# One more small transfer behind the load of x: four pieces of 16384 bytes on ScalarE's DMA queue, in a decode kernel fed by SyncE's queue

## The chip, the cores and the metric

The kernel runs on one core of one Trainium2 chip. The time is the device time of one execution in microseconds (us), taken from the runs without and with a profile; the span is the time from the first to the last instruction of the profiled execution. The core has five engines with queues of their own: TensorE (PE), VectorE (DVE), ScalarE (ACT), GpSimd (POOL) and SyncE (SP). SP and ACT can issue DMA transfers; all of the core's transfers run on the same 16 DMA engines.

## What is computed

One decode step of a transformer block, for four sequences and one new token each: attention over the last 4096 positions of a cache, and a gated feed-forward. All inputs are bfloat16.

```python
# B, Sq, D = 4, 1, 576; 32 query heads, 16 key heads of 128; caches of 16384 positions
def _A_ref(x, k_cache, v_cache, wq, wo):
    q = (x @ wq) -> [B, 32, 1, 128]
    k = k_cache[:, :, Sk - 4096:, :] ; v = v_cache[:, :, Sk - 4096:, :]   # each key head serves 2 query heads
    p = softmax(q k^T * 128 ** -0.5)
    return (p v) @ wo
def _B_ref(x, W_gate, W_up, W_down):        # F = 4608
    gate = x @ W_gate ; up = x @ W_up
    return (relu(gate) * up) @ W_down
h  = x + _A_ref(layernorm(x), ...)
h2 = h + _B_ref(layernorm(h), ...)
```

## The kernel before

The window of K and V is 16 x 4 heads of one MB each, 67 MB for K and the same for V. The kernel walks over it in 16 *quads*: a quad is four key heads of one sequence, 4 MB of K and 4 MB of V. A quad lies in SBUF as 128 partitions of 32768 bytes. The buffer `pool` has four slots for quads. Every load of the kernel but that of x is issued by SP, in an order written out by hand (`transfers`): wq in two parts, K0, K1, V0, K2, V1, ... V15, then wo, W_gate, W_up and six pieces of W_down. Ahead of each issue SP waits for the instruction that last used the place in `pool`: K for the last transpose of an earlier quad (`TR`), V for the last product with probabilities (`PV`). L273, L278, L283, L285, L292, L295, L297 and L303 are the lines of these loads.

For a quad i, VectorE transposes K in four parts into `kT`, a buffer of its own with `NKT = 4` places of 8192 bytes in each partition (`tr`, L451); each part waits for the load of K and for the scores that last used that place of `kT` (`QK`). TensorE forms the scores of the part (`qk`, matmuls recorded at L513 and L515), VectorE takes the maximum (`rmax`), ScalarE the exponential (L386), VectorE transposes the probabilities (`trp`), and TensorE multiplies them with V (`pv`). The order on each engine is the program's own order; TensorE's part is a loop over pairs of quads.

At the start ScalarE issues the load of x (L339), then waits for the variance of x and takes its root (L340). POOL fills constants, VectorE makes identity matrices and normalises x, TensorE multiplies it with wq, and the result is laid out for the scores. Behind the attention come the product with wo, the second normalisation, gate and up, and the product with W_down, whose last pieces are waited for one after the other.

A transfer's name, `land("x")` for that of x, stands for its semaphore: an instruction with that name among its `deps` waits until all of it has landed. Transfers with different keys have semaphores of their own.

Of the kernel before, what the change touches and what calls it, by code (L numbers as in the profile page):

```python
# [10 lines left out]
BF16 = mybir.dt.bfloat16  # L11
# [138 lines left out]
def bass_sequential_preLN__sliding_block_cached__glu_gated_reglu__decode_kernel(  # L150
# [12 lines left out]
    with ExitStack() as es:  # L163
        cnt = [0]

        def sb(name, shape, dt):
            return es.enter_context(nc.sbuf_tensor(name, shape, dt))

        pool = sb("pool", [128, NSLOT * QUAD], BF16)
        kT = sb("kT", [128, NKT, QUAD // 8], FP32)  # L170
# [74 lines left out]
        S = Sched()  # L245
# [55 lines left out]
        for k, (f0, f1) in enumerate(WD):  # L301
            transfers.append((("wd", k), f"wd{k}", ["ATTN"],
                              lambda e, f0=f0, f1=f1: e.dma_start(  # L303
                                  out=pool[:, f0 * D:f1 * D], in_=B_W_down.rearrange("(p j) n -> p (j n)", j=JJ)[:, f0 * D:f1 * D])))
# [4 lines left out]
        def land(name):  # L309
            return ("L",) + (name if isinstance(name, tuple) else (name,))  # L310
# [26 lines left out]
        def prog_act(S):  # L337
            a = "scalar"
            S.dma(a, lambda e: e.dma_start(out=x_bf[:, :], in_=A_x.rearrange("b s d -> (b s) d")), "x", name=land("x"))  # L339
            S.op(a, lambda e: e.activation(out=st1[:, 14:15], in_=st1[:, 13:14], func=ACT.Sqrt, bias=eps_c[0:B, 0:1], scale=1.0),  # L340
                 deps=["D_VAR", "EPS"], name="A_STD")
            S.op(a, lambda e: e.copy(out=dup[:, :].rearrange("p (r u) -> p r u", u=2),
                                     in_=bass.AP(tensor=ident_b, offset=0, ap=[[128, 64], [1, 64], [0, 2]])), deps=["IDB"], name="DUP")
            S.op(a, lambda e: e.copy(out=col[:, :].rearrange("p (a s) -> p a s", s=NS),
                                     in_=bass.AP(tensor=ident_b, offset=0, ap=[[128, NS], [0, 128], [1, NS]])), name="COL")
# [3 lines left out]
                                           in_=bass.AP(tensor=ident_b, offset=0, ap=[[128, NS], [0, 16], [1, NS], [0, 2]]),  # L349
# [4 lines left out]
                                     in_=bass.AP(tensor=mask, offset=0, ap=[[NHQ, 128], [0, 16], [1, NHQ]])), deps=["M0"], name="SAME")  # L354
            for u in range(2):
                S.op(a, lambda e, u=u: e.activation(out=xn4[:, u, 0:B], in_=pb[STB][:, 0:B], func=ACT.Copy, scale=par[:, u:u + 1]),
                     deps=["XDUP", "PAR2", "XN4Z"], name=f"XN4{u}")
            for k in range(2):
                S.op(a, lambda e, k=k: e.copy(out=q_bf[:, k, :].rearrange("p (x e k) -> p x e k", e=2, k=32),
                                              in_=pb[QB[k]].rearrange("p (x k e) -> p x e k", e=2, k=32)), deps=["QMM"], name=f"QBF{k}")  # L360
            S.op(a, lambda e: e.copy(out=qrep[:, :, :].rearrange("p x (g y) -> p x g y", g=4),  # L361
                                     in_=sc.ap().rearrange("p (g r) -> p g r", g=4)[:, :, 0:128].rearrange("p g (x y) -> p x g y", x=4)),
                 deps=["QREP"], name="D_QR")
# [16 lines left out]
            for i in range(NQUAD):  # L380
                S.op(a, lambda e, i=i: e.activation(out=diag[:, i % 2, :], in_=spot[:, :], func=ACT.Copy, scale=rmx[:, i % 2:i % 2 + 1]),  # L381
                     deps=[("RMAX", i), "SPOT"], name=("DIAG", i))
                deps = [("BIAS", i)]
                if i >= 2:
                    deps.append(("TRP", i - 2))
                S.op(a, lambda e, i=i: e.activation(  # L386
                    out=Pb[:, (i % 2) * 1024:(i % 2 + 1) * 1024], in_=sc[:, (i % 2) * 1024:(i % 2 + 1) * 1024], func=ACT.Exp,
                    scale=SCALE, bias=bias[:, i % 2:i % 2 + 1], accum_out=rs1[:, i:i + 1]),
                    deps=deps, name=("EXP", i), inc=7 if i == NQUAD - 2 else 1)
                if i + 2 < NQUAD:  # L390
                    qzero(i + 2)
            S.op(a, lambda e: e.copy(out=bass.AP(tensor=spread, offset=0, ap=[[16 * H, H], [4 * H + 1, 4], [4, H]]),
                                     in_=bass.AP(tensor=ident_b, offset=0, ap=[[128, H], [0, 4], [1, H]])),
                 deps=["SP0"], name="SPREAD")
            S.op(a, lambda e: e.copy(out=oX[:, :, :].rearrange("p e b -> p (e b)"), in_=pb[0][:, 0:EO * B]), deps=["OSEL"], name="OX")  # L395
            S.op(a, lambda e: e.activation(out=st2[:, 14:15], in_=st2[:, 13:14], func=ACT.Sqrt, bias=eps_c[0:B, 0:1], scale=1.0),
                 deps=["D_VAR2"], name="A_STD2")
            S.op(a, lambda e: e.copy(out=hnT[0:64, 4, 0:B], in_=tpv[0:64, 16:20]), deps=["TP2", "HN4Z"], name="N1")
            S.op(a, lambda e: e.copy(out=hnT[:, 0:4, 0:B], in_=tpv[:, 0:16].rearrange("p (c b) -> p c b", b=B)), name="N2")
            for u in range(2):  # L400
                S.op(a, lambda e, u=u: e.activation(out=hn4[:, u, 0:B], in_=pb[SUB][:, 400:400 + B], func=ACT.Copy, scale=par[:, u:u + 1]),
                     deps=["HDUP"], name=f"HN4{u}")
            for k, (f0, f1) in enumerate(CUTS):
                S.op(a, lambda e, k=k, f0=f0, f1=f1: e.activation(out=gate_sb[:, :, f0:f1].rearrange("p j f -> p f j"), in_=part(0, k, "f j"), func=ACT.Relu),
                     deps=[("GATE", k)], name=("RELU", k))
# [3 lines left out]
        def prog_dve(S):  # L409
# [12 lines left out]
            for k in range(5):  # L422
                w = 1 << k
                S.op(v, lambda e, w=w: e.tensor_scalar(out=num[:, w:2 * w], in0=num[:, 0:w], scalar1=float(w), scalar2=None, op0=ALU.add),
                     deps=["NUM0"] if k == 0 else [("NUM", k - 1)], name=("NUM", k))
            S.op(v, lambda e: e.transpose(out=numT[:, :], in_=num[:, :]), deps=[("NUM", 4)], name="NUMT")
            for k in range(4):
                S.op(v, lambda e, k=k: e.tensor_tensor(out=ident_b[32 * k:32 * k + 32, 32 * k:32 * k + 32], in0=num[32 * k:32 * k + 32, :],
                                                       in1=numT[32 * k:32 * k + 32, :], op=ALU.is_equal),
                     deps=["NUMT", "P0"] if k == 0 else [], name="IDB" if k == 3 else None, signal=k == 3)  # L430
# [4 lines left out]
                 name="PAR2")  # L435
# [6 lines left out]

            def tr(i, j):
                f = 4 * i + j
                deps = [land(("K", i))]
                if f >= NKT:
                    deps.append(("QK", f - NKT))
                x0 = at[("K", i)] + j * (QUAD // 4)
                src = pool[:, x0:x0 + QUAD // 4].bitcast(FP32).rearrange("p (t c k) -> p c t k", c=2, k=32)
                dst = kT[:, f % NKT, :].rearrange("p (c t k) -> p c t k", c=2, k=32)  # L450
                S.op(v, lambda e: e.transpose(out=dst, in_=src), deps=deps, name=("TR", f), inc=3 if f == 5 else 1)  # L451
# [12 lines left out]
            def own(w):  # L464
# [8 lines left out]
                                              in_=bass.AP(tensor=ident_f, offset=0, ap=[[128, 128], [0, 2], [64, 2], [1, NHQ], [NHQ, 8]]),  # L473
                                              axis=AX.X, op=ALU.add), deps=["IDF", "G0"], name="GATH")
            for i in range(NQUAD):
                for j in range(4):
                    tr(i, j)
                    if j == 0 and i > 1 and i % 2 == VLEAD:
                        own(i // 2 - 1)
                rmax(i)  # L480
                fbias(i)
                trp(i)
# [8 lines left out]
                 deps=["RS", "EXT"], name="NORM")  # L491
# [3 lines left out]
            for k, (f0, f1) in enumerate(CUTS):  # L495
                S.op(v, lambda e, k=k, f0=f0, f1=f1: e.tensor_tensor(out=hh[:, :, f0:f1], in0=part(1, k, "j f"), in1=gate_sb[:, :, f0:f1], op=ALU.mult),
                     deps=[("GU", k), ("RELU", k)], name=("HH", k))
            for j in range(2):
                j0, j1 = j * JJ // 2, (j + 1) * JJ // 2
                S.op(v, lambda e, j0=j0, j1=j1: e.transpose(out=hhT[:, j0:j1, :].rearrange("p j b -> p (j b)"),  # L500
                                                            in_=hh[:, j0:j1, :].rearrange("p j f -> p (j f)")),
                     deps=[("HH", len(CUTS) - 1)], name=("HHT", j))
# [3 lines left out]
        def prog_pe(S):  # L506
# [135 lines left out]
            for k, (f0, f1) in enumerate(WD):  # L642
                deps = [land(("wd", k))]
                for f in range(f0, f1):
                    if f % (JJ // 2) == 0:
                        deps = deps + [("HHT", f // (JJ // 2))]
                    for u in range(2):
# [3 lines left out]
                        deps = []  # L651

        progs = [("gpsimd", prog_pool), ("sync", prog_sync), ("scalar", prog_act), ("vector", prog_dve), ("tensor", prog_pe)]
        S.begin(False)
        for _, p in progs:
# [36 lines left out]
```

## Time and profile before

| | before |
|---|---|
| median of 3 runs | 377.70 us (377.58 to 377.77) |
| the profiled execution | 377.95 us |
| its span | 376.6 us |
| PE / DVE / ACT / POOL busy | 307.4 / 226.6 / 53.4 / 6.1 us |
| read from HBM | 159.58 MB, 424 GB/s over the span |
| granted TensorE clock | 0.918 |
| load of a quad, issue to landing (median) | 27.3 us |

The profile is of one execution on the chip. A row names the engine, the line of the kernel, the operation and its tiles; a "q" behind an engine's name (SPq, ACTq) is its sequencer, which issues DMA transfers. All positions in time are counted from the start of the span. "DMA" in the chain of waits means that the chain's next step waited for a transfer to land. Besides the rows, the trace holds a record of every DMA packet with its start, duration, size and queue (not the DMA engine that ran it), and the time of each increment of a transfer's semaphore.

### The profile page before, as it was taken

The numbers are of one execution on the slowest core, as the hardware profiler recorded it, in microseconds if no ns is written. First come the engines' busy times: TensorE is split into PE (matmuls) and PEld (weight loads), VectorE is DVE, ScalarE is ACT, GpSimd is POOL, SyncE is SP. The second block draws the span as 40 slices with busy tenths as digits, with TensorE's granted clock in tenths as the row PEclk, the third lists the DMA queues.
The fourth block names the chain that finished last, engine by engine and source line by source line (L and its number), as shares of the span: only waits on it lengthen the run. The fifth ranks groups of instructions, "written<-read, shape, count | busy, mean of one in ns | idle before, by whom it ended". The sixth has DMA issues, their size and how long they took to land.

```text
span 376.6 us, 2757 instructions
## 1 busy us (share of the span) xinstructions
PE 307.4 (82%) x1454; PEld 74.0 (20%) x778; DVE 226.6 (60%) x165; ACT 53.4 (14%) x140; POOL 6.1 (2%) x16
## 2 busy tenths in 40 slices
PE   0439999959995999599959996899679977986677
PEld 0102221212121212022201221122112211222214
DVE  8255849494839492949475758675677658222230
ACT  2231220202020202002200211021102010101020
POOL 6000000000000000000000000000000000000000
PEclk9959999989998999589976999899989998996988
DMA  8999999999999999999999999999999999999995
GB/s 335 445 444 432 404 445 445 425 412 442 442 421 421 442 445 432 407 442 445 432 411 439 445 432 414 435 445 432 414 435 445 432 418 435 433 421 435 442 399 237
DMA packets 6501, 159.66 MB, mean 424 GB/s; under 512 B 728, under 2 KB 864, under 8 KB 1632
## 3 DMA queue, kind: packets, MB, share of 16 engines
q1 hardware_dynamic: 6488, 159.59, 98.8%
q8 instruction: 3, 0.05, 0.1%
q14 instruction: 2, 0.02, 0.0%
q10 hardware_dynamic: 8, 0.00, 0.0%
HBM read 159.58 MB, written 0.00 MB: 424 GB/s over the span
## 4 chain that ended last, share of the span: by engine, by line
DMA 60%; DVE 27%; PE 11%; ACT 1%; SPq 1%; issue 0%; DVEq 0%
DMA pool<-in_A_k_cache_dram 55%; DVE kT L451 20%; DMA pool<-in_B_W_down_dram 5%; DVE acc L468 4%; PE sc L513 3%; PE sc L515 3%; DVE P L465 2%; PE val L513 2%; PE val L515 2%; PE pb L513 1%; DVE o_bf L489 0%; ACT L386 0%; DVE probT L462 0%; DVE rmx L454 0%; ACT P L386 0%
## 5 line engine op out<-in xcount | busy, mean ns | idle before, releaser
L451 DVE STREAM_TRANSPOSE kT<-pool 128x2048 f32<-128x2048 f32 x64 | 142.7, 2279 | 20.2 <-DMA pool<-in_A_k_cache_dram 20.1
L513 PE MATMUL sc<-kT,qz 128*128 128x512 bf16 x256 | 109.2, 426 | 40.3 <-DVE kT L451 40.2
L513 PE MATMUL val<-pool,probT 128*64 128x512 bf16 (+2 forms) x344 | 111.2, 374 | 3.1 <-DMA pool<-in_B_W_down_dram 3.1
L515 PE MATMUL sc<-kT,qz 128*128 128x512 bf16 x256 | 108.3, 423 | 0.0
L515 PE MATMUL val<-pool,probT 128*64 128x512 bf16 x272 | 103.1, 379 | 0.0
L513 PEld LDWEIGHTS sc<-kT,qz 128*128 128x128 bf16 x256 | 26.3, 103 | 149.5 <-DVE kT L451 77.1
L513 PEld LDWEIGHTS val<-pool,probT 128*64 128x64 bf16 (+1 forms) x344 | 34.1, 107 | 89.1 <-issue 77.6
L454 DVE TENSOR_REDUCE rmx<-sc 128x1 f32<-128x1024 f32 x16 | 19.6, 1225 | 38.5 <-PE sc L515 38.5
L381 ACT ACTIVATE diag<-spot,rmx 128x16 f32<-128x16 f32 x16 | 4.9, 307 | 242.5 <-DVE rmx L454 242.5
L462 DVE STREAM_TRANSPOSE probT<-P 128x1024 bf16<-128x1024 bf16 x16 | 19.9, 1245 | 20.5 <-ACT P L386 20.5
L386 ACT ACTIVATE P<-sc,bias 128x1024 bf16<-128x1024 f32 x16 | 17.8, 1115 | 18.7 <-DVE bias L457 18.7
L375 ACT COPY qz<-qrep 32x128 bf16<-32x128 bf16 x64 | 18.8, 293 | 0.6
L457 DVE TENSOR_REDUCE bias<-pb 128x1 f32<-128x16 f32 x16 | 2.8, 175 | 22.0 <-PE pb L513 22.0
L465 DVE TENSOR_TENSOR P<-val,mask 128x1024 f32<-128x1024 f32 x8 | 9.5, 1190 | 10.6 <-PE val L515 10.6
L468 DVE TENSOR_REDUCE acc<-P 128x128 f32<-128x1024 f32 x8 | 15.2, 1898 | 0.3
L513 PE MATMUL sc<-pool,oX 128*4 128x288 bf16 x32 | 9.4, 324 | 0.4 <-ACT oX L395 0.4
L515 PE MATMUL sc<-pool,oX 128*4 128x288 bf16 x32 | 9.4, 324 | 0.0
L525 PE MATMUL pb<-ident_b,xn_bf 4*128 4x4 bf16 (+1 forms) x5 | 0.4, 179 | 10.7 <-DVE xn_bf L419 10.7
L492 DVE TENSOR_TENSOR h_row<-sc,x_bf 4x576 f32<-4x576 f32 x1 | 0.7, 746 | 11.0 <-PE sc L515 11.0
L513 PE MATMUL sc<-col,foe 4*128 4x512 bf16 x16 | 6.3, 397 | 1.2 <-ACT qrep L361 1.2
L513 PEld LDWEIGHTS pb<-diag,same 128*128 128x128 f32 x32 | 4.8, 188 | 10.0 <-ACT diag L381 10.0
L513 PE MATMUL pb<-diag,same 128*128 128x16 f32 x32 | 6.3, 273 | 0.0
(103 smaller groups left out, 79.1 us busy)
## 6 DMA issues: line engine op xcount, KB each, us to landing
pool<-in_A_k_cache_dram SPq DMA_DIRECT2D x16, 4096.0 KB, 27.3
pool<-in_A_v_cache_dram SPq DMA_DIRECT2D x16, 4096.0 KB, 27.3
pool<-in_A_wo_dram SPq DMA_DIRECT2D x1, 4608.0 KB, 18.4
pool<-in_B_W_gate_dram SPq DMA_DIRECT2D x1, 4608.0 KB, 19.9
pool<-in_B_W_up_dram SPq DMA_DIRECT2D x1, 4608.0 KB, 23.2
pool<-in_A_wq_dram SPq DMA_DIRECT2D x1, 4096.0 KB, 12.6
pool<-in_B_W_down_dram SPq DMA_DIRECT2D x1, 2016.0 KB, 13.7
pool<-in_B_W_down_dram SPq DMA_DIRECT2D x1, 1296.0 KB, 16.5
```

Source lines behind the costliest of these rows:

```text
L375: S.op(a, lambda e, src=src, dst=dst: e.copy(out=dst, in_=src), deps=deps, name=("QZ", i) if g == 3 else None, signal=g == 3, inc=8 if i = ...
L381: S.op(a, lambda e, i=i: e.activation(out=diag[:, i % 2, :], in_=spot[:, :], func=ACT.Copy, scale=rmx[:, i % 2:i % 2 + 1]), deps=[("RMAX", ...
L386: S.op(a, lambda e, i=i: e.activation(out=Pb[:, (i % 2) * 1024:(i % 2 + 1) * 1024], in_=sc[:, (i % 2) * 1024:(i % 2 + 1) * 1024], func=ACT ...
L451: S.op(v, lambda e: e.transpose(out=dst, in_=src), deps=deps, name=("TR", f), inc=3 if f == 5 else 1)
L454: S.op(v, lambda e: e.tensor_reduce(out=rmx[:, i % 2:i % 2 + 1], in_=sc[:, (i % 2) * 1024:(i % 2 + 1) * 1024], axis=AX.X, op=ALU.max), dep ...
L457: S.op(v, lambda e: e.tensor_reduce(out=bias[:, i % 2:i % 2 + 1], in_=pb[TPB][:, 16 * (i % 2):16 * (i % 2) + 16], axis=AX.X, op=ALU.min), ...
L462: S.op(v, lambda e: e.transpose(out=pT[i % NPT], in_=Pb[:, (i % 2) * 1024:(i % 2 + 1) * 1024]), deps=[("EXP", i)] + ([("PV", i - NPT)] if ...
L465: S.op(v, lambda e: e.tensor_tensor(out=own_sb[:, :].rearrange("p (x d) -> p x d", d=DH), in0=val[:, :].rearrange("p (x d) -> p x d", d=DH ...
L468: S.op(v, lambda e: e.tensor_reduce(out=acc[:, w, :], in_=own_sb[:, :].rearrange("p (x d) -> p d x", d=DH), axis=AX.X, op=ALU.add), deps=[ ...
L492: S.op(v, lambda e: e.tensor_tensor(out=h_row[:, :], in0=attn, in1=x_bf[:, :], op=ALU.add), deps=["ATTN", land("x")], name="H")
L513: return e.matmul(o, lhsT=l, rhs=r, start=start, stop=stop, skip_group_check=skip)
L515: return e.add_instruction(mybir.InstMatmult(name=nc.get_next_instruction_name(), start_tensor_calc=start, stop_tensor_calc=stop, bass_ski ...
```

## The change

Right behind the load of x, ScalarE issues one more transfer. It reads the first eight rows of wq (8 x 8192 bytes) as four pieces of 16384 bytes, and writes them to partitions 0, 8, 16 and 24 of `kT`, over its first two places. The first transpose into `kT` waits for it in addition; it and the second one then overwrite these bytes, and nothing reads them.

```diff
         def prog_act(S):
             a = "scalar"
             S.dma(a, lambda e: e.dma_start(out=x_bf[:, :], in_=A_x.rearrange("b s d -> (b s) d")), "x", name=land("x"))
+            S.dma(a, lambda e: e.dma_start(
+                out=kT[0:32:8, 0:2, :].rearrange("p f n -> p (f n)").bitcast(BF16), in_=A_wq[0:8, :].rearrange("(a c) n -> a (c n)", c=2)),
+                "stagger", name=land("stagger"))
             S.op(a, lambda e: e.activation(out=st1[:, 14:15], in_=st1[:, 13:14], func=ACT.Sqrt, bias=eps_c[0:B, 0:1], scale=1.0),
                  deps=["D_VAR", "EPS"], name="A_STD")
...
             def tr(i, j):
                 f = 4 * i + j
-                deps = [land(("K", i))]
+                deps = [land(("K", i))] + ([land("stagger")] if f == 0 else [])
                 if f >= NKT:
                     deps.append(("QK", f - NKT))
```

## The prediction

> **What bounds the kernel now.** I read the share of the span by engine, then the DMA queues, the chain that ended last, the work by stages, and the waits of SP. Besides these views I used the trace's single records of DMA packets (start, duration, size, queue) and of semaphore increments; I name them where I use them.
>
> The queues of the page first:
>
> ```profile
> q1 hardware_dynamic: 6488, 159.59, 98.8%
> q8 instruction: 3, 0.05, 0.1%
> q14 instruction: 2, 0.02, 0.0%
> q10 hardware_dynamic: 8, 0.00, 0.0%
> HBM read 159.58 MB, written 0.00 MB: 424 GB/s over the span
> ```
>
> SP's queue (q1) fills the sixteen DMA engines for 98.8% of the span. The 8 packets of q10 are the load of x: by the records four of 1152 bytes and four of 4 bytes (semaphore increments), so a transfer of four rows runs on four engines. q8 and q14 fetch instructions through the same engines; they matter below.
>
> The work by stages (PE, PEld, DVE, ACT, POOL busy, then clock, DMA share, GB/s):
>
> ```profile
> 24.00:120.00 96.00, 84.65 (x348) 19.26 (x179) 67.47 (x42) 14.20 (x36) 0.00 (x0) 0.94 1.00 431
> 120.00:220.00 100.00, 89.20 (x356) 19.94 (x183) 67.74 (x42) 12.92 (x35) 0.00 (x0) 0.90 1.01 434
> 220.00:320.00 100.00, 84.15 (x347) 19.21 (x179) 66.76 (x42) 11.86 (x31) 0.00 (x0) 0.95 1.00 431
> ```
>
> No stage of the attention loop leaves the DMA engines idle. The packets of 32768 bytes take 1217.7 ns on average and 1211 at the least (4224 records), which is 16 x 32768 / 1.2177 = 430.6 GB/s: the rate of the stages. The stream is bounded packet by packet on each engine.
>
> The end of the chain:
>
> ```profile
> 353.06 0.33 SPq L303
> 353.43 0.43 SPq L303
> 353.90 0.43 SPq L303
> 354.38 18.94 DMA pool<-in_B_W_down_dram
> 373.36 0.70 PE val L513 x7
> 374.08 0.68 PE val L513 x5
> 374.78 0.42 DVE out_sb L503
> ```
>
> The last piece of W_down ends the kernel. Was the stream ever dry? The small up load is issued at 337.74 and takes 24.1 us, to 361.8; the down loads are issued from 353.06, 8.8 us before that. A K or V load takes 27.3 us from issue to landing where its bytes need 8 x 1.2177 = 9.7 us. So the queue always holds more, and a delay of about a microsecond in compute is hidden.
>
> Only one thing remains: when does the **slowest** engine finish? The increments answer it. The last down piece lands on the sixteen engines at 0 to 0.31 us (ten engines), 0.53, 0.57, 1.01, 1.75, 1.87 and 1.97 us after the first. Three engines are late. At each of them the records show a fetch: q8 packets of 16384 bytes at 24.4, 329.7 and 362.4 us of the span stand in a gap of 0.96, 1.08 and 1.07 us in one engine's q1 packets, and the next packet there is 0.47 us longer than its like. Each costs its engine 1.43 to 1.55 us. Later loads keep the delay: the latest engine is 1.69 us behind the first at 102.7 us and still at 297.0 us.
>
> **The change part by part.** The four pieces are shaped as x is: four rows, so four engines, one packet of 16384 bytes each (64 KB in all).
>
> (1) Bytes on four engines. By size a piece costs half of a 32768-byte packet: 1.213 / 2 = 0.61 us on each of the four engines, on the other twelve nothing. The nearest row for a strange packet inside a full stream is q8's, of the same size: 1.43 to 1.55. I take 0.61, because the source and target are those of ordinary loads and the packet arrives when the stream begins (SP's first load is issued at 0.73 us, and this one at about 1.3). Both ends are kept: 0.61 to 1.55. A gain from the bytes themselves is excluded: nothing is taken away.
>
> (2) Where this goes. An engine that gets 0.61 us more and is not one of the three late ones still finishes in front of them: room is 1.97 - 0.57 = 1.40 us for twelve engines and 1.97 - 1.01 = 0.96 for the thirteenth. So the end moves by 0 unless one of the late three is among the four. Which are they? By the packet records, q1 begins on the sixteen engines one after the other within 0.49 us. I followed the late engines back, packet to packet (the next begins 3 to 4 ns ahead of the end of the last); all three lead to engines that began tenth or later. Ties of a nanosecond leave this uncertain. If four rows go to the engines that are served first, the late ones are spared. The Trainium skill, "DMA: Bandwidth & Descriptors", section "Why a DMA increments its semaphore by 16 and not by 1", says that a transfer on k engines uses the lowest-numbered k; the same page, "Latency and other measured facts", says that engines 7 and 15 are usually the slower ones. No record here carries an engine's number; by both rules the end would move by 0.
>
> (3) The issue on ScalarE's queue:
>
> ```profile
> 0.73 0.55 ACTq L339 DMA_DIRECT2D x_bf<-in_A_x_dram  x1
> 1.38 1.28 ACT L340 ACT_TABLE_LOAD   x1 [1.38 <-POOL xn L327]
> 8.43 0.29 ACT L340 ACTIVATE st<-st,eps_c 4x1 f32<-4x1 f32 x1 [5.77 <-DVE st L415]
> ```
>
> A second issue of 0.55 us pushes the table load from 1.38 to about 1.93, over at 3.2; the next ACT work waits until 8.43 for DVE. 5.77 us of idle time cover it: cost 0. Without that cover it would be 0.55 us. x is issued ahead of it and is not delayed.
>
> (4) The new wait on DVE, ahead of the first transpose into kT (L451). That transpose starts at 23.64, when K0 lands; the pieces are issued at 1.3 and need 1 to 2 us. The semaphore is long up, and one passed wait is left. DVE's next transposes queue behind it, and PE's first scores behind those; cost 0 to some hundredths of a us, covered as below.
>
> (5) The first loads on the four engines: wq and K0 land up to 0.61 us later (1.55 at the far end). Q's matmuls, V0's issue (16.81) and the first transpose (23.64) move with them. What comes late is the issue of the load freed at 49.22, which lands 24.4 us after its issue where its bytes need 9.7. 14.7 us of queue cover it. Without that queue the whole 0.61 would count.
>
> Sum: profiled span 376.6, plus 0 = 376.6; with the 1.35 us that lie around the span, 377.95 as profiled. The runs shown have a median of 377.70, 0.25 lower; against them the forecast is 377.7. A change of 0.2%, 0.76 us, is about what a measurement of this kernel can tell from none.
>
> **The rivals.**
>
> *A late engine is among the four* (slower). Place: the last landing at 374.4. It decides as soon as one of the three carries a piece. Price 0.61 by bytes: 378.3, within 0.2%. At q8's price 1.55: 379.25. It counts as slower above 0.76; the middle, 1.08, gives 378.8. For it: drawn blind, four of sixteen miss all three late engines in only 12 x 11 x 10 / (16 x 15 x 14) = 39% of cases. Against it: the tracing back in (2).
>
> *Shifting four engines by half a packet loosens the stream* (faster). If the engines hinder each other because they walk in step, packets could fall from 1217.7 towards 1211 ns: 264 packets of 32768 bytes on each engine x 6.7 ns = 1.8 us at most; half of it gives 376.8. For it: all engines keep one pace over 194 us. Against it: that pace is the same for engines at 0, 0.5, 1.0 and 1.7 us of offset, and single engines already walk far out of step without going faster. The Trainium skill, "DMA: Bandwidth & Descriptors", section "Latency and other measured facts", reports that copies with a row pitch of 4 MiB halve in rate, and infers streams in lock-step on the same channel. K's heads lie 16384 x 128 x 2 bytes = 4 MiB apart, but the trace has 431 to 434 GB/s and nothing near a half; so hardly any of that is there to be won.
>
> *The change doesn't do what it says*: the transfer is spread over all sixteen engines. Then 4 KB each, 1.213 / 8 = 0.15 us on every engine, the late ones too: 377.85.
>
> **How the numbers follow.** Hidden behind the late engines: 0.56, at 377.7. A late engine hit: 0.26, at 378.3 to 379.25. Loosened stream: 0.12, at 376.8 in the middle. Spread over sixteen: 0.06, at 377.85. Slower by over 0.2%: 0.18 of the 0.26, as most prices between the ends lie above 0.76, and 0.05 of the first case, for the first stage's irregular packets (127 of 992 above 1230 ns between 25 and 101 us) growing with the shift: 0.23. Faster: 0.12. Within 0.2%: 0.65. The range takes half of the loosened case at the bottom, 377.0, and the greater part of the hit case at the top, 378.9.
>
> **What would show it.** q10 has 16 packets instead of 8, four of them of 16384 bytes, in the first 4 us. The increments of K1 and later loads show four engines 0.6 us further back and the same three last. The first transpose starts up to 0.6 us later, the last landing stays at 374.4. I am wrong if the last landing moves: by 0.6 or more, then a late engine was hit; forward, with packets nearer 1211 ns, then the stream was loosened; or if the fetches fall on other engines or cost something else.

## The result, and the profile after

| | before | after |
|---|---|---|
| median of 22 runs each | 377.75 us (377.55 to 379.48) | 378.44 us (378.02 to 380.39) |
| ratio after / before | | 1.0022, 95% interval 1.0012 to 1.0031 |
| the profiled execution, its span | 377.95, 376.6 us | 378.52, 377.2 us |
| last landing of W_down, from the span's start | 374.39 us | 374.99 us |
| first landing of K0, spread over the sixteen engines | 23.12 us, 0.50 us | 23.76 us, 1.55 us |

The change costs 0.69 us. That is little, but the interval of the ratio leaves no room for "no change": the forecast of 377.7 was wrong, and the time lies in the upper part of its range. In what follows a difference is that of the medians of one comparison; the ratio is taken round by round on one chip. The two mostly agree within 0.2 us, but not always: the ratio says 0.6 us where the medians say 0.32 (sixteen pieces), and 1.6 us where they say 1.11 (partitions 0 to 3).

The page of after first, its DMA queues:

```profile
q1 hardware_dynamic: 6488, 159.59, 98.7%
q10 hardware_dynamic: 16, 0.07, 0.1%
q8 instruction: 3, 0.05, 0.1%
q14 instruction: 2, 0.02, 0.0%
HBM read 159.65 MB, written 0.00 MB: 423 GB/s over the span
```

The stream is the same 6488 packets. q10 has eight packets more: by the records four of 16384 bytes and four increments. The change does what it says, on four engines.

The same three stages of the attention loop (PE, PEld, DVE, ACT, POOL busy, then clock, DMA share, GB/s):

```profile
24.00:120.00 96.00, 84.18 (x349) 19.20 (x179) 67.02 (x41) 15.30 (x40) 0.00 (x0) 0.97 1.00 431
120.00:220.00 100.00, 88.48 (x356) 19.82 (x183) 68.75 (x42) 12.93 (x35) 0.00 (x0) 0.91 1.00 431
220.00:320.00 100.00, 84.51 (x339) 19.13 (x175) 66.54 (x41) 11.85 (x31) 0.00 (x0) 0.91 1.01 433
```

Nothing has changed here: the rate is 431 to 433 GB/s, as before. The time is lost before 24 us, and then carried to the end. The end of the chain of waits of after (start, length, what; us):

```profile
354.70 0.33 SPq L303
355.08 0.43 SPq L303
355.55 0.43 SPq L303
356.03 17.93 DMA pool<-in_B_W_down_dram
374.00 1.36 PE val L516 x12
375.38 0.42 DVE out_sb L506
```

The chain has the same members. The last twelve matmuls end at 375.36 instead of 374.76, and the span is 0.6 us longer. What moved is the last landing, by 0.60 us, and nothing was added behind it. The increments of this last piece come at 0 to 0.43 us (nine engines), 0.75, 1.56, 1.69, 1.70, 1.76, 1.81 and 2.11 us after the first: one engine alone is now last, where three late ones stood close together before.

The start of the same chain, before and then after:

```profile
1.65 21.96 DMA pool<-in_A_k_cache_dram
23.64 2.32 DVE kT L451
```

```profile
1.65 23.66 DMA pool<-in_A_k_cache_dram
25.34 2.32 DVE kT L454
```

The first load of K lands for the first transpose 1.70 us later, not the 0.61 that the pieces' bytes explain. The rates of the first stage, 4 to 10 us of the span, before and then after, in the view of the work by stages:

```profile
4.00:10.00 6.00, 0.00 (x0) 0.00 (x0) 5.72 (x17) 1.00 (x3) 2.60 (x7) 1.00 1.02 437
```

```profile
4.00:10.00 6.00, 0.00 (x0) 0.00 (x0) 5.72 (x17) 1.00 (x3) 2.60 (x7) 1.00 0.98 377
```

The last number falls from 437 to 377 GB/s, while the DMA share hardly falls: the engines are as busy, but move less. The records say how. The pieces' packets begin at 5.88, 6.21, 6.22 and 7.32 us and take 611, 611, 611 and 796 ns. The 32 KB packets of wq that begin between 5.7 and 8.1 us take 1264 to 1765 ns, one 2055, where most take 1213 in before: 0.59 us of extra time on the mean of the sixteen engines, called the **stall** below. It is not on the four engines alone: the first landing of the last piece of W_down, which is that of an engine without a piece, comes at 372.88 instead of 372.43. Engines that carry a piece are behind by more: K0's offsets are 0 to 0.40 us on twelve engines, then 0.71, 0.95, 1.07 and 1.55.

ScalarE's queue and engine in the timeline of after:

```profile
1.35 0.68 ACTq L340 DMA_DIRECT2D kT<-in_A_wq_dram  x1
2.12 1.28 ACT L343 ACT_TABLE_LOAD   x1 [2.12 <-POOL xn L327]
8.43 0.29 ACT L343 ACTIVATE st<-st,eps_c 4x1 f32<-4x1 f32 x1 [5.03 <-DVE st L418]
```

The issue pushes the table load to 2.12, and the next work still begins at 8.43. Nothing is lost here.

### The profile page after: what moved, and what is told of

The parts are those of the page before. It is cut to its first block, busy times and chain, and to the rows that moved or that the text cites. A ratio compares the mean times of both kernels' runs of the same rounds, so it can differ in the third digit from the quotient of the medians.

```text
span 377.2 us, 2759 instructions
## 1 busy us (share of the span) xinstructions
PE 308.5 (82%) x1454; PEld 74.1 (20%) x778; DVE 226.6 (60%) x165; ACT 53.4 (14%) x140; POOL 6.1 (2%) x16
## 3 DMA queue, kind: packets, MB, share of 16 engines
q1 hardware_dynamic: 6488, 159.59, 98.7%
## 4 chain that ended last, share of the span: by engine, by line
DMA 54%; DVE 29%; PE 14%; ACT 1%; SPq 1%; issue 0%; DVEq 0%
DMA pool<-in_A_k_cache_dram 49%; DVE kT L454 21%; DMA pool<-in_B_W_down_dram 5%; PE sc L516 4%; DVE acc L471 4%; PE sc L518 4%; PE val L516 3%; DVE P L468 2%; PE val L518 2%; DVE probT L465 1%; ACT P L389 1%; PE pb L516 1%; DVE o_bf L492 0%; ACT L389 0%; DVE rmx L457 0%
## 5 line engine op out<-in xcount | busy, mean ns | idle before, releaser
L474 DVE STREAM_TRANSPOSE qT<-q_bf 128x1024 bf16<-128x1024 bf16 x1 | 1.2, 1245 | 9.8 <-ACT q_bf L362 9.8
## 6 DMA issues: line engine op xcount, KB each, us to landing
pool<-in_B_W_down_dram SPq DMA_DIRECT2D x1, 2016.0 KB, 12.7
```

Source lines behind the costliest of these rows:

```text
L474: S.op(v, lambda e: e.transpose(out=qT[:, :], in_=q_bf[:, :, :].rearrange("p k x -> p (k x)")), deps=["QBF1"], name="D_QT")
```

## The experiments

In the diffs the two operands of the added transfer stand on lines of their own, and only what changes is shown. All are against the changed kernel, unless "before" is named. For each run the text gives the difference from before, the ratio with its interval, and the last landing (374.39 in the profiled execution of before, 374.99 after). A landing or a stall is that of one profiled execution. The stall is the mean, over the sixteen engines, of the time by which the 32 KB packets of q1 exceed 1213 ns while the pieces run.

**First: is it the bytes, their place, or the wait?** The source was the first suspect for the stall: the pieces read rows of wq that the stream reads at the same time.

*Another source*, outside the window of K:

```diff
-in_=A_wq[0:8, :].rearrange("(a c) n -> a (c n)", c=2)
+in_=A_k_cache[0, 0, 0:256, :].rearrange("(a c) d -> a (c d)", a=4)
```

> The four pieces have the same size, targets, queue and wait as in the change, but are read from 64 KB of the K cache outside the window, which no other load reads, instead of the first rows of wq. Theory 1 (late engine: the pieces hold up only their four engines, two of which also fetch instructions on q14 and so finish last): nothing changes, 0.6 to 0.7 us above before (378.4). Theory 2a (all sixteen engines stall while the pieces run, because both queues read wq at once): the packets of 32768 bytes between 5 and 9 us stay near 1213 ns instead of 1400 to 1750, and the first engine's landing of K0 comes 0.6 us earlier than with the change; time 0.0 to 0.3 us above before. Theory 2b (any second queue with data stalls all): as with the change, 378.4, packets up to 1700 ns.

Measured: 378.33, +0.62, ratio 1.0013 (1.0005 to 1.0022); last landing 374.79. The stall is nearly gone (0.15 us), and the rate of the first stage recovers to a good part:

```profile
4.00:10.00 6.00, 0.00 (x0) 0.00 (x0) 5.72 (x16) 1.00 (x3) 2.60 (x7) 1.00 0.99 415
```

Yet the end is nearly as late as after. So here it is not the stall of all sixteen that costs the time at the end; K0's spread, 1.05 us, shows single engines still behind by more than 0.61. And the pieces did not run together this time (two at 6.0 and 6.3, two at 7.1 us), so that the source wasn't the only difference.

*Sixteen pieces of 4096 bytes*, the same 64 KB:

```diff
-out=kT[0:32:8, 0:2, :], in_=A_wq[0:8, :].rearrange("(a c) n -> a (c n)", c=2)
+out=kT[0:128:8, 0, 0:1024], in_=A_wq[0:8, :].rearrange("a (c n) -> (a c) n", c=2)
```

> The same 64 KB of wq on the same queue, in sixteen pieces of 4096 bytes to sixteen partitions, so that all sixteen engines share them. Theory 1 (late engine): each engine gets 4096 / 32768 of 1.21 us, 0.15 us, the late ones too; the end moves by 0.15, time 377.9, and the spread of K0's landing stays near 0.4 us. Theory 2a and 2b (stall of all while 64 KB pass): the stall is that of the change, 0.4 to 0.6 us on all engines, time 378.2 to 378.4, with packets above 1400 ns in the wq stage.

Measured: 378.03, +0.32, 1.0016 (1.0005 to 1.0026). The stall is 0.08, K0's spread 0.43, the last landing 374.38. Against the next run, whose pieces have almost no bytes, the landing is 0.16 later, which is the price by bytes (0.15); the medians say twice that and the ratio four times, so its size stays open. The spread of the pieces does away with the single late engines, but not with the bytes.

*Four pieces of 64 bytes*, with the same wait and the same issue:

```diff
-out=kT[0:32:8, 0:2, :], in_=A_wq[0:8, :].rearrange("(a c) n -> a (c n)", c=2)
+out=kT[0:32:8, 0, 0:16], in_=A_wq[0:8:2, 0:32]
```

> Four pieces of 64 bytes instead of 16384, same queue, partitions and wait; only the bytes are gone. Theory 1 and theory 2a: no measurable difference from before, within 0.15 us of 377.75. Theory 2b in the form that the second queue itself (its descriptors, its wait) costs, not its bytes: 0.3 to 0.7 us above before. It also shows what the issue on ScalarE's queue and the wait ahead of the first transpose cost by themselves; expected 0.

Measured: 377.69, -0.02, 1.0001 (0.9992 to 1.0010); last landing 374.22. Neither the issue, nor the wait, nor four more packets cost anything. All of the change's cost is in the bytes or in where they go.

*Pieces of twice the size*:

```diff
-out=kT[0:32:8, 0:2, :], in_=A_wq[0:8, :].rearrange("(a c) n -> a (c n)", c=2)
+out=kT[0:32:8, 0:4, :], in_=A_wq[0:16, :].rearrange("(a c) n -> a (c n)", c=4)
```

> Four pieces of 32768 bytes, twice the change, into all four places of the buffer. Theory 1 (late engine): the four engines lag by 1.2 to 2 us at K0 instead of 0.4 to 1.2, the last of them is 0.6 us later at the end than with the change: 379.0 to 379.2, the first engines' landings unmoved against the change. Theory 2 (stall of all): the first engine's landing of K0 moves too, by about another 0.6 us, and the time is 379.0 or more with a spread at the end that grows less than 0.6.

Measured: 379.32, +1.61, 1.0046 (1.0033 to 1.0059); stall 0.88, last landing 375.65. Doubling adds 0.92, which is more than the 0.61 us by bytes.

**Second: how many engines, and when?**

*Two pieces*, from K's cache:

```diff
-out=kT[0:32:8, 0:2, :], in_=A_wq[0:8, :].rearrange("(a c) n -> a (c n)", c=2)
+out=kT[0:16:8, 0:2, :], in_=A_k_cache[0, 0, 0:128, :].rearrange("(a c) d -> a (c d)", a=2)
```

> Two pieces of 16384 bytes instead of four, read from the K cache outside the window as in the run with the other source, so they use two DMA engines. Revised theory 1: what ends the kernel later is the piece on an engine that later also runs an 8 KB instruction fetch (q14); in the runs so far both such engines were among the four. If neither is among the first two, the end stays within 0.15 us of before (377.7 to 377.85), and two increments of K0 lie 0.6 to 1 us back while the last three of the last landing are the engines of the 16 KB fetches. If one is among them, 378.2 to 378.4, the same as with four pieces. Rival (any second-queue data on any engine costs the end in proportion): half of the 0.62 us of four pieces, 378.0.

Measured: 377.88, +0.16, 1.0005 (0.9996 to 1.0014); last landing 374.23. Not told apart from no change, although one engine with an 8 KB fetch is among the two, for which 378.2 to 378.4 was expected. K0's offsets show 1.04 and 1.11 on two engines. Between the loads that land at 72 and 81 us one of them meets an 8 KB instruction fetch (q14): followed packet by packet, it loses 0.69 us and goes from 1.06 to 1.75. The other engine with such a fetch carries no piece and goes from 0.46 to 1.46. At the end the first is at 1.85, only just in front of the late ones at 1.89 to 2.01.

*The same pieces, issued later*, behind two activations on ScalarE, at 11.78 instead of 1.35 us, so that they run in the stream of K0, at 15.7 to 17 us (the diff is against before, the wait ahead of the first transpose is that of the change):

```diff
             S.op(a, ...)   # the two activations that write xn
+            S.dma(a, lambda e: e.dma_start(
+                out=kT[0:32:8, 0:2, :], in_=A_wq[0:8, :].rearrange("(a c) n -> a (c n)", c=2)),
+                "stagger", name=land("stagger"))
```

> The transfer of the change, rows 0 to 7 of wq, but issued on ScalarE behind L359, at about 12.5 us of the span, so that it runs while K0 streams and not while wq does. Revised theory 1 (late engine): the four engines still lag by 0.6 to 1.1 us and the end comes 0.5 to 0.65 us above before, 378.2 to 378.35, as with the other source. Theory 2a (both queues reading wq make all sixteen stall): packets stay at 1213 to 1300 but on the four engines, and the first landing of the later K loads is 0.3 to 0.4 us earlier than with the change. If the stall of all engines comes from the transfer's place at the start rather than from wq, it is gone here as well, and only the run with other rows tells.

Measured: 378.35, +0.63, 1.0017 (1.0008 to 1.0026); stall 0.43, last landing 374.82. By then the stream had left wq. So "both read wq" falls, and so does "it is the first packets of the stream".

*Other rows of wq*:

```diff
-in_=A_wq[0:8, :]
+in_=A_wq[256:264, :]
```

> The change, but the four pieces are read from rows 256 to 263 of wq instead of 0 to 7, at the same time of the span. Theory 2a in the form same tensor (lock-step with the stream of wq): packets of all engines near 1500 ns on average between 5 and 9 us, as in the change, 378.4. In the form same rows (both read the same 64 KB): no such stall, as with the other source; time still 378.3 through the late engine. The late engine is expected in both.

Measured: 378.45, +0.73, 1.0017 (1.0008 to 1.0026); stall 0.41, last landing 374.88. The same cost from rows that the stream reads at another time: the source's place is not it.

*Before, with the last piece of W_down in two transfers*, partitions 0 to 87 and 88 to 127, so that the late engines might be spared:

```diff
+        PARTS = {len(WD) - 1: ((0, 88), (88, 128))}
-                                  out=pool[:, f0 * D:f1 * D], ...
+                                  out=pool[p0:p1, f0 * D:f1 * D], ...
```

> The kernel before, without the pieces; only the last piece of W_down (1152 bytes for each of 128 partitions) is split in two transfers, partitions 0 to 87 and 88 to 127, which should run on 11 and on 10 engines instead of 16. If the end is set by the engines of the 16 KB instruction fetches and these are not among the eleven, those engines are spared 8 packets of about 53 ns, the others carry 12 instead of 8: the last landing comes 0.3 to 0.4 us earlier, 377.3 to 377.45. If a late engine is among the eleven: 0.1 to 0.3 us later than before, 377.8 to 378.0. If the end isn't set by the slowest engine at all: no change, 377.7.

Measured: 378.05, +0.33, 1.0003 (0.9993 to 1.0013): no gain. The last piece now lands early, at 373.58 and 373.78, but the two in front of it land at 373.71 and 374.38 instead of 373.32 and 374.03, and the last 14 matmuls wait for these. It gave something else: the first part has increments of eleven engines, and they end at 373.58, while the three with the 16 KB fetches are at 373.99 to 374.38 with the piece before: none of the three is among the eleven. So a transfer of four rows misses these three, if it takes the first of the same engines: this step of the prediction held.

**Third: the law of sizes, the source again, and taking load off the late engines.**

*Half the size*:

```diff
-out=kT[0:32:8, 0:2, :], in_=A_wq[0:8, :].rearrange("(a c) n -> a (c n)", c=2)
+out=kT[0:32:8, 0, :], in_=A_k_cache[0, 0, 0:128, :].rearrange("(a c) d -> a (c d)", a=4)
```

> Four pieces of 8192 bytes, read from the K cache outside the window; half of the bytes of the run with the other source. Revised theory 1 (late engine, with a threshold): the two engines that also run the 8 KB fetches lie about 0.75 and 1.1 us behind the first without any piece, and half a piece adds 0.3 to 0.5 us; 1.1 + 0.5 = 1.6 is less than the 1.75 to 1.97 of the engines with the 16 KB fetches, so the end moves by less than 0.15 us: 377.65 to 377.85. Rival (the cost goes with the bytes): half of 0.62, 378.0.

Measured: 377.81, +0.10, 0.9998 (0.9989 to 1.0007); last landing 374.42. For these targets, pieces below some size between 8 and 16 KB are hidden.

*A third source*, wo:

```diff
-in_=A_wq[0:8, :].rearrange("(a c) n -> a (c n)", c=2)
+in_=A_wo.rearrange("r n -> (r n)")[0:32768].rearrange("(a c) -> a c", a=4)
```

> Four pieces of 16384 bytes as in the change, read from the first 64 KB of wo, a weight that no other load reads at that time. If the stall of all sixteen engines comes from pieces out of wq alone, packets stay as with the K cache (0.15 us of excess on average over the engines between 4.5 and 8 us); if from pieces out of any weight, 0.4 to 0.6 us of excess. Revised theory 1 expects the end at 378.3 to 378.45 in both cases, since the engine that ends last is one with a piece.

Measured: 378.39, +0.68, 1.0016 (1.0006 to 1.0025); stall 0.38. (Its profiled execution lies 1.5 us above its median, so only its start is read; the last landing in it, 374.54, does not explain that time.) wo is read by the stream 300 us later, and the cost is the same as from wq.

*Twice the size from K's cache*:

```diff
-out=kT[0:32:8, 0:2, :], in_=A_wq[0:8, :].rearrange("(a c) n -> a (c n)", c=2)
+out=kT[0:32:8, 0:4, :], in_=A_k_cache[0, 0, 0:512, :].rearrange("(a c) d -> a (c d)", a=4)
```

> Four pieces of 32768 bytes, read from the K cache outside the window, so that they surely overlap each other in time. Revised theory 1: an engine with piece and 8 KB fetch lies 1.1 plus 1.3 to 1.8 us behind the first, 2.4 to 2.9, and the end comes 0.7 to 1.2 us above before, 378.4 to 378.9. If the stall of all sixteen needs only that four pieces run at once, it shows here too (first landing of K0 0.4 us or more later than with the tiny pieces) and the time is that of the doubled change, 379.3; if it needs wq as source, it doesn't.

Measured: 379.60, +1.89, 1.0046 (1.0032 to 1.0060); stall 0.91, last landing 375.86; more than expected. With longer pieces the overlap is certain, and the stall from K's cache is as large as from wq (0.88). The source is out. The increments show what is late at the end: between the loads that land at 62 and 82 us, offsets of 1.48 and 1.65 become 2.35 and 2.46. The jump is that of the two 8 KB fetches of q14; without bytes (the run with 64 bytes a piece) the same jump leads to 0.73 and 1.09. **Both engines with an 8 KB fetch carry a piece.**

*Before, with wq's last part in three transfers* (partitions 0 to 63, 64 to 107, 108 to 127), to move bytes between engines at the start:

```diff
+        SHARE = ((0, 64), (64, 108), (108, 128))
-            lambda e, o: e.dma_start(out=o, in_=A_wq[512:576, :]...)
+            ... for h, (p0, p1) in enumerate(SHARE): e.dma_start(out=pool[p0:p1, ...], in_=...[p0:p1, :])
```

> The kernel before, without pieces; the first load (the last 64 rows of wq, 4096 bytes for each of 128 partitions) is split by partitions 0 to 63, 64 to 107 and 108 to 127, which should run on 16, 11 and 10 engines: engines 11 to 15 then move 4 packets of 159 ns instead of 8, the first ten 10. If the three engines of the 16 KB fetches are among the last five, they lie 0.6 us less behind and the others 0.3 us more: the last landing comes 0.3 to 0.6 us earlier, 377.2 to 377.45. If the end isn't set by these engines, or the split costs the start more than it brings: 377.7 or later.

Measured: 379.46, +1.75, 1.0047 (1.0033 to 1.0062). It says nothing of the balance: the issues put SP's next load of wq from 1.20 to 2.30 us, and that delay of the whole stream covers anything else.

*The same split for a late load*, the small part of W_up, in before and in after:

```diff
+        SHARE = ((0, 64), (64, 108), (108, 128))
+        for h, (p0, p1) in enumerate(SHARE):
+            transfers.append((("wu4", h), f"wu4_{h}", made[2], ... out=pool[p0:p1, wu4:wu4 + HALF], ...
```

> The kernel before, without pieces; only the small load of W_up (4608 bytes for each of 128 partitions) is split by partitions 0 to 63, 64 to 107 and 108 to 127, so that engines 11 to 15 move 4 packets of 178 ns instead of 8 and the first ten 10; it is queued 8 us ahead of its turn, so the start and the queue are not touched. Theory (the slowest engine sets the end, and in before these are the three with the 16 KB fetches, none of them among the first eleven): the three lie 0.7 us less behind, the others 0.36 more; the last landing moves from 1.75 to 1.97 behind the first engine's old place to 1.3 to 1.5: 377.25 to 377.5. If the slowest engine doesn't set the end, 377.7; if the split has a side effect as at the tail, 377.8 to 378.1.

> The same split of W_up's small load, but in the kernel with the change. Theory: here the last engine is one of the four with a piece, the lowest-numbered ones, and the split gives it two packets of 178 ns more: 0.36 us later than the change, 378.7 to 378.9. The sign is opposite to that in before. If the engines with the 16 KB fetches ended last here as well, it would be 0.3 to 0.5 us earlier than the change, 377.95 to 378.15.

Measured: 380.99, +3.17, 1.0081 (1.0068 to 1.0095) in before; 382.58, +4.76, 1.0126 (1.0110 to 1.0141) in after. Both are far from what was expected. The stage in which this load runs, in before and then in the split version of before:

```profile
356.50:363.50 7.00, 6.79 (x109) 1.49 (x41) 0.00 (x0) 2.80 (x7) 0.00 (x0) 0.76 0.98 412
```

```profile
356.50:363.50 7.00, 5.97 (x86) 1.46 (x38) 0.69 (x2) 2.48 (x7) 0.00 (x0) 0.76 0.97 246
```

412 GB/s become 246 at the same DMA share: the sign of the stall again, without any piece. In this stage the packets of 4608 bytes take 350 ns (median, at most 547) instead of 179. A load split by partitions ran at little more than half the rate. That pointed at the target.

The split version of after says one more thing. Up to this load it is the changed kernel, with the same pieces from the same rows, and yet its stall is 0.19 instead of 0.59. Its pieces begin at 6.29, 7.04, 7.07 and 7.09 us, those of after at 5.88, 6.21, 6.22 and 7.32. With one set of targets the stall therefore varies from execution to execution.

**Fourth: the targets.**

*Three pieces*, at partitions 0, 8 and 16:

```diff
-out=kT[0:32:8, 0:2, :], in_=A_wq[0:8, :].rearrange("(a c) n -> a (c n)", c=2)
+out=kT[0:24:8, 0:2, :], in_=A_k_cache[0, 0, 0:192, :].rearrange("(a c) d -> a (c d)", a=3)
```

> Three pieces of 16384 bytes from the K cache outside the window, so on three engines. Two pieces gave 0.16 us above before, four gave 0.62. Theory: with two pieces one engine of the 8 KB fetches is hit, with four both; the one that comes last in the four-piece run decides. If it is the third, 378.2 to 378.35 as with four; if it is the fourth, 377.85 to 377.95 as with two. A cost in proportion to the bytes would give 378.15.

Measured: 377.82, 0.00, 1.0000 (0.9991 to 1.0009); last landing 374.14. Both expectations were too high. One engine is 0.94 behind at K0, and one with an 8 KB fetch ends at 1.28, still in front of the late three (1.75 to 1.77). It takes the fourth piece to push an engine past them.

*The same pieces to partitions 0, 4, 8 and 12*; size, source, queue, issue and wait as in the change:

```diff
-out=kT[0:32:8, 0:2, :]
+out=kT[0:16:4, 0:2, :]
```

> The change with other target partitions: 0, 4, 8 and 12 instead of 0, 8, 16 and 24; bytes, source, queue, engines and wait are the same. Theory of the writing side (the pieces and the running stream meet in groups of four partitions, each of which one engine fills in the quad loads; the first four engines then own 0 to 3, 4 to 7, 8 to 11 and 12 to 15): no engine meets another, the packets of the sixteen stay near 1213 ns while the pieces run, each piece costs its engine 0.61 us by its bytes, an engine with piece and 8 KB fetch ends at 1.1 + 0.6 = 1.7 us behind the first, no later than the engines of the 16 KB fetches (1.75 to 1.97), and the time is 377.7 to 377.9: what the prediction forecast for the change itself. The Trainium skill, SBUF: State Buffer, section on the DMA port swizzle, gives these groups of four partitions and a port for each. Rival (four large pieces at once stall all engines wherever they are written): 378.3 to 378.45, as with the change.

Measured: 377.77, -0.05, 1.0002 (0.9989 to 1.0014).

```profile
4.00:10.00 6.00, 0.00 (x0) 0.00 (x0) 5.72 (x17) 1.00 (x3) 2.60 (x7) 1.00 1.00 426
```

426 GB/s against 377. The four pieces take 611 ns each, of the 97 packets of 32 KB that begin between 5 and 12.7 us 93 take 1213 and the longest 1284, and K0's offsets are 0.59, 0.66, 0.67 and 0.68 on four engines: near the price by bytes, 0.61, as the prediction had it. (Its profiled execution is 0.7 us above its median, with slower packets between 16 and 62 us; only the start is read.)

*The same pieces to partitions 0, 1, 2 and 3*:

```diff
-out=kT[0:32:8, 0:2, :]
+out=kT[0:4, 0:2, :]
```

> The change with the four pieces written to partitions 0, 1, 2 and 3. Theory of the writing side: four engines and the stream's own writer meet in one group of partitions; the pieces take about four times as long as by their bytes, 2.4 us, and the four engines lag by 1.5 to 2.5 us at K0: with the 8 KB fetches 2.6 to 3.6 at the end, time 378.6 to 379.6. Rival (target doesn't matter): 378.3 to 378.45, as with the change.

Measured: 378.93, +1.11, 1.0042 (1.0026 to 1.0058); last landing 375.41.

```profile
4.00:10.00 6.00, 0.00 (x0) 0.00 (x0) 5.72 (x17) 1.00 (x3) 2.60 (x7) 1.00 0.86 350
```

The worst of the three: the pieces take 725 to 973 ns, the sixteen packets of q1 beside them 2207 to 2536, and the stall is 1.24 us. The time was expected, the path was not: the pieces were to take 2.4 us and their engines to be 1.5 to 2.5 us behind at K0; they are 0.67 to 1.15 behind, and it is all sixteen that are late. One thing besides the targets differs: the issue takes 0.26 instead of 0.68 us, and the pieces begin at 3.40 us, beside the first 32 KB packets of wq, not at 5.9.

The Trainium skill, "SBUF — State Buffer", section "Door 1: The DMA port swizzle (why `[64,N]` ≈ `[32,N]`)", says that four neighbouring partitions share a port of the memory, sixteen ports in all, and that a transfer's rate hangs on how many of them its partitions reach; "DMA: Bandwidth & Descriptors", section "The descriptor swizzle", gives each engine one port in a transfer to all partitions. If the four engines are the first four, 0, 4, 8 and 12 are their own ports; of 0, 8, 16 and 24 three are other engines' ports; 0 to 3 are all one. The stalls, 0.05, 0.59 and 1.24 us, come in that order, and the 350 ns against 179 above agree with it too. No record carries a port, so that the runs show the dependence on the targets, and the ports are the Trainium skill's explanation of it. They do not settle when the stall is large: it is 0.15 to 0.59 in the runs with 0, 8, 16 and 24, and three pieces to 0, 8 and 16, all begun at 7.05 to 7.09 us, took 611 ns each with a stall of 0.05. The times depend on the targets more steadily than the stalls: five versions with four pieces of 16384 bytes to 0, 8, 16 and 24 cost 0.62 to 0.73 us, the one to 0, 4, 8 and 12 nothing that is measured.

*Twice the size to 0, 4, 8 and 12*:

```diff
-out=kT[0:32:8, 0:2, :], in_=A_wq[0:8, :].rearrange("(a c) n -> a (c n)", c=2)
+out=kT[0:16:4, 0:4, :], in_=A_wq[0:16, :].rearrange("(a c) n -> a (c n)", c=4)
```

> Four pieces of 32768 bytes from wq to partitions 0, 4, 8 and 12. Theory of the writing side: 1.21 us on four engines and nothing on the others; an engine with piece and 8 KB fetch ends at 1.1 + 1.2 = 2.3 us behind the first, 0.35 to 0.55 us after the engines of the 16 KB fetches: 378.05 to 378.35, the first landing of K0 at 23.1 to 23.4 us. Rival (target doesn't matter): as the doubled change, 379.3, with the first landing of K0 at 24.2.

Measured: 378.26, +0.44, 1.0016 (1.0006 to 1.0025); stall 0.06, pieces 1213 to 1224 ns, last landing 374.75. The end of its chain:

```profile
356.44 17.26 DMA pool<-in_B_W_down_dram
373.74 1.37 PE val L516 x12
375.14 0.41 DVE out_sb L506
```

Almost without a stall, 1.21 us on four engines do show at the end, where 0.61 did not. No rule of collisions is needed for this: only the room of an engine that the prediction left out of account.

**The sum that fits.** With 64 bytes a piece the late three land at 374.22 at the latest, and the later of the two engines with an 8 KB fetch at 372.48 + 1.18 = 373.65 (first landing and its offset). Room: 0.57 us. What the pieces cost this engine is read at K0, 350 us ahead of the end; 23.46 stands for the landing of K0 with 64 bytes a piece, a value about the middle of the sixteen (23.31 to 23.66), so that a sum holds to some 0.1 us. The end should be the later of two: the late three, and 373.65 plus that cost:

| targets, bytes a piece | cost on that engine | it lands, by the sum | the late three land | last landing, measured |
|---|---|---|---|---|
| 0, 8, 16, 24; 16384 (after) | 1.37 (K0 at 23.76 + 1.07, against 23.46) | 375.02 | 374.57 to 374.69 | 374.99 |
| 0 to 3; 16384 | 1.73 (24.49 + 0.7, against 23.46) | 375.38 | to 375.39 or 375.41 | 375.41 |
| 0, 4, 8, 12; 32768 | 1.21 (by bytes) | 374.86 | to 374.21 | 374.75 |
| 0, 4, 8, 12; 16384 | 0.61 (by bytes) | 374.26 | | the median is that of before |

For after, 1.07 is the offset of the engine that goes to 2.06 between 72 and 82 us. The engine was picked by what it does later, so the table shows that the numbers agree and is no forecast.

The late three carry no piece, as far as the increments can be followed, and yet the stall moves them. In after they land at 374.57 to 374.69; they would have been last, 0.30 us after before's 374.39, even without the fourth engine, which adds another 0.30. With targets 0 to 3 the stall makes the whole price: the late three are as late as the engine of the sum, so this row is no test of it. The row with 32768 bytes is: there the late three stand where they do with 64 bytes, and the engine with piece and fetch alone passes them.

## Why the prediction was wrong, by its own steps

- **Step (1) failed in its size, and its reason was wrong.** It took 0.61 us a piece because "the source and target are those of ordinary loads". The target is not: the targets 0, 8, 16 and 24 cost the engine that decides 1.37 us, of which about 0.4 is the stall that all sixteen have (first landing of the last piece at 372.88, against 372.48 with 64 bytes), and with 0, 4, 8 and 12 the 0.61 came out. The other end of its bounds, 0.61 to 1.55, from the q8 rows, was the nearer one. The argument that the packet arrives when the stream begins weighed nothing: issued ten us later, the pieces cost the same.
- **Step (2) looked at the wrong engines.** It was right that the last landing decides and that the three late engines are not among the four. But it said that the end moves only if one of them is among the four; in after they carry no piece and land up to 0.30 us later all the same. And it priced the room of the thirteenth engine, 0.96, against 0.61 alone, and didn't ask what made this engine 1.01 late: an 8 KB fetch, of which it had two in the page's line of q14. Both engines with such a fetch are among the four. 1.37 on a room of 0.57 to 0.96 must show; the room itself varies, since the same engine lay 1.01 back in before and 1.18 with 64 bytes a piece. Even at 0.61 the margin was near nothing. No record carries an engine's number; what made engines late here were instruction fetches.
- **The stall of the other twelve engines was not foreseen at all**: step (1) puts it at nothing ("on the other twelve nothing") because its price was by bytes. It made the first transpose 1.70 us late, above the 0.61 to 1.55 of step (5). Its cover held as step (5) said for the work that waits on it: the loop's rate is unchanged. For the end it is one of two ways to the same price: in after it moves the late three by 0.30 us, while the run from K's cache, whose engines with pieces are late and which has hardly a stall, is about as slow (+0.62 and +0.69).
- **Step (3) held**: the table load moved from 1.38 to 2.12, 0.19 more than said, and the next ACT work stayed at 8.43.
- **Step (4) held for a wrong reason.** The wait costs nothing (377.69 with 64 bytes). But the pieces do not "need 1 to 2 us": they land at 8.7 to 10.1 us. They are still 13 us ahead of K0.
- **The rivals.** The slower rival had its direction and its price right (378.3 to 379.25), but its engines wrong: none of the three with a 16 KB fetch carries a piece; an engine that was fourth from the end overtook them. That its price range held the measured 378.44 is in this sense luck. The stream was not loosened: mean packet between 36 and 300 us 1217.2 ns, before 1217.3. The transfer was not spread over sixteen engines; made so, it cost 0.32 by the medians.
- **Left open:** how four small writes slow down all sixteen engines, and why the stall is 0.59 in one execution and 0.19 in another. The packets lengthen together, in after by 50 to 550 ns (one by 842); no run separates the reason. Nor was it tried which engine writes which partition, one by one. No version beat before: with targets 0, 4, 8 and 12 the change is free, and brings nothing.

## What to carry to other kernels

In a stream that keeps all DMA engines full, the end is that of one engine: list for each engine everything it carries beside the stream, instruction fetches too, and measure a small addition against the room of *that* engine, not against the mean. A small transfer's price is not its bytes alone: the partitions that it writes can decide between nothing and a microsecond. When the DMA share stays and GB/s falls, as from 437 to 377 here, the engines are busy but hinder each other; in this case other targets brought 426 back, so they are the first thing to try.

## What the runs showed of the hardware that was not expected

- A second queue's transfer waits long when the first queue has filled the engines: issued at 1.35 us, even pieces of 64 bytes have their first packet at 5.82, and the first increment at 7.04, one q1 packet (1.2 us) behind it. In the run with targets 0 to 3, whose issue took 0.26 instead of 0.68 us, the first packet came at 3.40.
- Four pieces of the same size on the same queue can delay *all sixteen* engines, and which partitions they write matters: the stall is 0.05 us with 0, 4, 8 and 12, 0.15 to 0.59 with 0, 8, 16 and 24, and 1.24 with 0 to 3 (where the pieces also began earlier).
- A 4608-byte packet takes 179 ns (median) in a transfer to all partitions, and 350 in one that was split by partitions.
- An instruction fetch costs its DMA engine far more than its bytes: an 8 KB fetch takes 309 to 394 ns by its record, and puts its engine about 0.6 to 1.0 us back.
